# The last 64 queries of each pair as four-quarter fp32 score products, and a planner with other durations and another order

## The chip, the core and the metric

The kernel runs on one core of a Trainium2 chip. The metric is device time in microseconds (us). Five engines work side by side: TensorE (PE: matrix products; PEld is its loading of weights), VectorE (DVE), ScalarE (ACT), GpSimd (POOL) and SyncE (SP, which here issues DMA transfers). Each runs its own list of instructions in order and waits on semaphores for the others.

## The reference

Attention with pairwise averaged queries, then two mixer blocks. Only the attention stage is touched by the change.

```python
# q, k, v: (4, 8, 1152, 64) float32
q_pool = q.reshape(B, H, S // 2, 2, D).mean(axis=3)              # 576 queries
scores = scale * np.matmul(q_pool, k.transpose(0, 1, 3, 2))     # 576 x 1152
scores = scores - np.max(scores, axis=-1, keepdims=True)
attn = np.exp(scores)
attn = attn / (np.sum(attn, axis=-1, keepdims=True) + 1e-09)
attn_out = np.matmul(attn, v)
...
x = _moe_ref(x=x, **moe_kwargs)     # gelu, layer norm, gate over the sequence
return _moe2_ref(x=x, **moe2_kwargs)    # token mixing, then channel mixing
```

## The kernel before

**The work.** The 32 heads are taken as 16 pairs, two heads in the two halves of the 128 partitions. For each pair the queries (576 per head) and keys (1152 per head) are transposed on TensorE (`q_tr`, L459, and `k_tr`, L470, into the buffer `tt`). ScalarE and VectorE then split them into a high and a low fp32r part (`k_hi`, `k_lo`, `q_hi`, `q_lo`); a product is made of three passes, high by high, high by low and low by high.

The maximum of each query over its keys must be known before the exponentials. So the scores are computed twice. First (`scores`, L523, tile `s`) with queries on the output partitions: five tiles of queries, four of 128 and one of 64, by three groups of 384 keys, so 15 tasks of six products per pair. `rowmax` (L530, VectorE) reduces each to negated maxima `mx`. `least` (L537) combines the three groups, and the result is split into `nmz`, transposed (`nm_tr`, L553) and copied to `nmT`. Then (`turned`, L578, tile `sT`) with keys on the partitions, 9 tiles of 128 keys for each half of the queries: three passes and a fourth that adds the negated maximum. ScalarE takes the exponential (`expo`, L586, tile `e`), GpSimd adds the nine up (`total`, L592, tile `acc`), and TensorE multiplies them with the values (`av`, L601, tile `po`: fp32, one head in each column half). The column sums of `acc` (`sums`, L614, tile `pt`, fp32 too) give the denominators; ScalarE adds eps, VectorE takes the reciprocal (L625) and multiplies (L632).

**The order.** All tasks go into a `Plan`: each has an engine, a duration, predecessors, an urgency, and rings of buffers that it takes or gives back. The planner plays them forward with these durations and writes out each engine's order. TensorE's order is fixed by hand in `line()`; the planner only slips in weight transposes that have no place in it. Ring `s` is the one to watch: three PSUM buffers, shared by `tt`, `s` and `sT`. A task on TensorE that needs the next buffer waits until all readers of the buffer three tasks earlier are done.

TensorE works one pair ahead with the maxima: in the period of pair i it computes the turned scores of pair i, in six groups of three (T), and the 15 score tasks of pair i+1 (S) in five groups of three, each after a T group; values (A, three key tiles, so six fp32 products) follow one group behind. The key and query transposes (Q) of pair i+2 and the maxima's transpose (N) stand in the same period:

```python
out += at(*(("t", i, x, j) for j in range(3 * n, 3 * n + 3)))
out += maxima(i + 1, 3 * g, 3 * g + 3) if i else begin[g]
```

The fifth S group holds the 64-query tasks. In the front (pair 0) the order differs, since the maxima of pairs 0 and 1 must both be made there. Beside attention, VectorE, ScalarE and GpSimd convert weights for the later stages (`Piece`, steps `wz`, `wy`, `wd`; `wg` are transposed gate weights).

## Time and profile before

| | |
|---|---|
| Median of three runs | 1132.81 us (1127.57, 1132.81, 1132.83) |
| Profiled execution, its own time | 1127.43 us |
| Its span | 1125.6 us |
| Mean granted clock of TensorE over the span | 0.995 |
| Attention, to the first product of the next stage | 0 to 530.98 us |
| Later stages | 530.98 to 1125.6 us |

The profiled execution is one of its own, so its time stands beside the three. A task's cost on TensorE is best read as the time from its first product's start to that of the next task, since products overlap and the busy time of one includes its way through the array.

### The profile page before, as it was taken

The page shows a single profiled execution, that of the slowest core. Times are in us where ns is not written, and L with a number is a line of the kernel's source. Part 1 is how long each engine was busy: PE and PEld are TensorE (multiplying, and loading weights), DVE is VectorE, ACT ScalarE, POOL GpSimd, SP SyncE. Part 2 cuts the span into 40 slices and gives each one's busy share as a digit, 9 for nine tenths or more (in the row PEclk, how much of TensorE's full clock was granted, in tenths as well). Part 3 has the DMA queues.
Part 4 walks back from the last instruction along what each step waited for, and adds up shares of the span by engine and source line. Part 5 has one row for each costly group of instructions (what it writes and reads, how often), then busy time and mean ns, then how long its engine had stood idle before and what let it go on. Part 6 is the DMA issues. An engine that isn't in the chain of part 4 may idle for free.

```text
span 1125.6 us, 20953 instructions
## 1 busy us (share of the span) xinstructions
PE 1108.6 (98%) x8699; PEld 902.1 (80%) x8699; DVE 669.5 (59%) x884; ACT 464.8 (41%) x812; POOL 582.1 (52%) x423
## 2 busy tenths in 40 slices
PE   8999999999999999999999999999899999999998
PEld 6777777677777777776889999998888888888887
DVE  6778888877667687862878878875733202112121
ACT  2355556554544555545555544553434111111111
POOL 3688889988877788789274454431404202001000
PEclk8999999999999999999999999999999999999999
DMA  8322334334133433221721222126351100001010
GB/s 181 70 64 61 83 84 105 77 102 110 53 80 96 109 86 87 59 78 39 228 74 51 101 76 75 48 71 230 133 195 47 38 1 29 10 1 38 1 38 19
DMA packets 87918, 88.00 MB, mean 78 GB/s; under 512 B 42512, under 2 KB 71440, under 8 KB 86032
## 3 DMA queue, kind: packets, MB, share of 16 engines
q1 hardware_dynamic: 87824, 86.67, 26.6%
q8 instruction: 68, 1.11, 0.4%
q14 instruction: 26, 0.21, 0.1%
HBM read 66.70 MB, written 19.96 MB: 77 GB/s over the span
## 4 chain that ended last, share of the span: by engine, by line
PE 93%; DVE 4%; issue 1%; ACT 1%; DMA 1%; SPq 0%; DVEq 0%; ACTq 0%
PE sT L578 15%; PE po L601 13%; PE psc L1455 13%; PE po L1485 13%; PE s L523 11%; PE psO L1243 5%; PE psS L1194 4%; PE psV L1065 4%; PE psU L1165 4%; PE psK L1348 2%; PE tt L470 2%; PE psH L1372 2%; DVE mx L530 2%; PE pt L614 1%; PE tt L459 1%; PE tt L553 1%
## 5 line engine op out<-in xcount | busy, mean ns | idle before, releaser
L592 POOL TENSOR_TENSOR acc<-acc,e 128x576 f32<-128x576 f32 x224 | 320.4, 1430 | 71.0 <-ACT e L586 57.9
L530 DVE TENSOR_REDUCE mx<-s 128x2 f32<-128x768 f32 (+1 forms) x240 | 215.3, 945 | 95.6 <-PE s L523 95.6
L586 ACT ACTIVATE e<-sT 128x576 f32<-128x576 f32 x288 | 169.0, 652 | 88.0 <-PE sT L578 86.5
L578 PE MATMUL sT<-q,k 64*128 64x288 f32 x1728 | 166.0, 303 | 0.3
L578 PEld LDWEIGHTS sT<-q,k 64*128 64x128 f32 x1728 | 128.2, 184 | 42.3 <-DVE mx L530 15.6
L601 PE MATMUL po<-e,vn 128*64 128x288 f32 x1152 | 160.8, 414 | 0.0
L1341 DVE SCALAR_TENSOR_TENSOR gc<-psc,gc 128x512 fp32r<-128x512 f32 (+1 forms) x52 | 34.9, 671 | 208.3 <-ACT gc L1338 208.3
L523 PE MATMUL s<-k,q 64*128 64x384 f32 (+1 forms) x1440 | 146.0, 343 | 1.0 <-ACT q L479 0.7
L523 PEld LDWEIGHTS s<-k,q 64*128 64x128 f32 (+1 forms) x1440 | 110.0, 177 | 19.3 <-DVE mx L530 2.8
L1338 ACT ACTIVATE gc<-psc 128x512 fp32r<-128x512 f32 (+1 forms) x52 | 30.3, 582 | 219.0 <-PE psc L1455 209.3
L601 PEld LDWEIGHTS po<-e,vn 128*64 128x64 f32 x1152 | 74.3, 136 | 57.7 <-issue 17.1
L1485 PE MATMUL po<-wc,gc 128*128 128x512 f32 x408 | 99.7, 392 | 0.0
L1485 PEld LDWEIGHTS po<-wc,gc 128*128 128x128 f32 x408 | 76.4, 188 | 17.4
L578 PE MATMUL sT<-nmT,pick 64*128 64x288 f32 x576 | 85.3, 291 | 0.0
L625 DVE RECIPROCAL pt<-pt 128x288 f32<-128x288 f32 x32 | 62.8, 1962 | 30.4 <-ACT pt L621 30.2
L1194 PE MATMUL psS<-wsg,vn 128*128 128x288 f32 x448 | 60.9, 295 | 1.3 <-DVE gt L1220 1.3
L1194 PEld LDWEIGHTS psS<-wsg,vn 128*128 128x128 f32 x448 | 59.7, 188 | 1.7 <-DVE gt L1220 1.5
L1455 PE MATMUL psc<-x,wc 128*128 128x512 f32 (+1 forms) x288 | 59.1, 357 | 0.0
L257 POOL TENSOR_TENSOR vn<-gv,vn 128x512 fp32r<-128x512 f32 (+1 forms) x20 | 28.2, 1438 | 55.5 <-ACT vn L1155 55.1
L592 POOL TENSOR_TENSOR acc<-e 128x576 f32<-128x576 f32 x32 | 47.6, 1489 | 15.1 <-ACT e L586 14.9
L257 POOL TENSOR_TENSOR ws<-wz,ws 128x512 fp32r<-128x512 f32 x24 | 32.7, 1374 | 43.8 <-ACT ws L323 43.7
L1455 PEld LDWEIGHTS psc<-x,wc 128*128 128x128 f32 x288 | 47.8, 188 | 8.9
(131 smaller groups left out, 1730.9 us busy)
## 6 DMA issues: line engine op xcount, KB each, us to landing
ws<-in_moe_w_ch_dram SPq DMA_DIRECT2D x24, 512.0 KB, 4.0
qn<-in_q_dram SPq DMA_DIRECT2D x32, 288.0 KB, 5.2
kn<-in_k_dram SPq DMA_DIRECT2D x32, 288.0 KB, 4.2
vn<-in_v_dram SPq DMA_DIRECT2D x32, 288.0 KB, 3.2
ac<-ws SPq DMA_DIRECT2D x32, 256.0 KB, 2.6
wc<-ac SPq DMA_DIRECT2D x6, 1024.0 KB, 7.9
out_dram<-ob SPq DMA_DIRECT2D x18, 256.0 KB, 2.0
ws<-in_moe_w_in_dram SPq DMA_DIRECT2D x8, 512.0 KB, 5.6
```

The costliest lines, as they stand in the source:

```text
L257: eng.tensor_tensor(out=out_, in0=in0, in1=in1, op=ALU.subtract)
L523: nc.tensor.matmul(ps[0:m, h, 0:KC], flat(c.q[x])[r, t * P:t * P + m], c.k[y][r, cs], start=(n == 0), stop=(n == 2))
L530: nc.vector.tensor_reduce(out=mx[i % 2][0:m, t, :, g], in_=ps[0:m, :, 0:KC], axis=AX.X, op=ALU.max, negate=True)
L578: nc.tensor.matmul(ps[:, h, 0:TC], left, right, start=(n == 0), stop=(n == 3))
L586: nc.scalar.activation(out=s.e[j], in_=ps[:, :, 0:TC], func=AF.Exp)
L592: eng.tensor_tensor(out=s.acc, in0=s.e[0] if j == 1 else s.acc, in1=s.e[j], op=ALU.add)
L601: nc.tensor.matmul(s.po[D * h:D * h + D, 0:TC], c.vn[:, h, j], s.e[j][:, h], start=(j == 0), stop=(j == J - 1))
L625: nc.vector.reciprocal(out=s.den, in_=s.den)
L1194: nc.tensor.matmul(ps[:, ch, 0:TC], V[sx][:, ti, db * P:(db + 1) * P], L.ws[sw][:, ti, ch * TC:(ch + 1) * TC], start=first, stop=end)
L1243: nc.tensor.matmul(ps[:, ch, 0:TC], L.wo[sw][:, db, cb * P:(cb + 1) * P], L.g[sx][:, db, ch * TC:(ch + 1) * TC], start=first, stop=end)
L1455: nc.tensor.matmul(ps, W[WC1[f // 4]][sw][:, cc, (f % 4) * P:(f % 4 + 1) * P], u[sx][:, cc], start=first, stop=end)
L1485: nc.tensor.matmul(pos[i, tt], g[i, f][sx][:, tt * P:(tt + 1) * P], W[WC2[f // 4]][sw][:, f % 4], start=(f == 0 and n == 0), stop=(f == NF ...
```

## The change

Four things change.

The three tasks for the last 64 queries of a pair become two. `quarters` computes them as plain fp32 products with 64 queries as the weights: two heads in the two row halves of TensorE, and two ranges of 288 keys in the two column halves, so each of the four products of a task uses one quarter. `quartermax` reduces 128 x 576 scores, and `least` first folds the two column halves of the maxima together. For these products ScalarE makes unsplit copies of the transposed keys (`k_all`, tile `kf`) and of the 64 queries (`q_all`, tile `qf`), from the same `tt` buffers as the split parts.

`line()` becomes strings, one letter for a task or a pair of transposes: the quarters (X) stand behind the third A of a period, ahead of the fourth T group, and the third T group has no S group behind it any more. Keys are transposed ahead of queries (before: after them, but for pair 0). Pair 0's order is written anew.

The split of the maxima goes to ScalarE (`nm_hi`) for all pairs, where before VectorE did it in `both` for all but pair 0. The planner gets other durations, with the part after which a unit is free told apart from the landing of the result (`land`), and other lags. That changes the order on VectorE, ScalarE and GpSimd. The warm-up on TensorE grows from 13 to 18 products.

```diff
@@ class Plan
+    STALL = 0.0
...
-                    if not line or line[0]["mode"] != "r" and "tr" not in line[0]["take"]:
+                    if not line or line[0]["mode"] not in ("r", "x") and "tr" not in line[0]["take"]:
...
+                if at > free.get("PE", 0.0) + 1e-6:
+                    t["end"] += self.STALL
@@ attention
         plan = Plan()
+        plan.LAG, plan.TURN, plan.STALL = 0.08, 0.17, 0.05
         marks = {}
-        for name, n in dict(s=3, po=1, tr=1, e=10, acc=3, qn=1, qs=1, kn=1, vn=2, k=3, q=3,
-                            nm=2, nmT=2, os=2, den=2).items():
+        for name, n in dict(s=3, po=1, tr=1, e=10, acc=3, qn=1, qs=1, kn=1, vn=2, k=3, q=3, kf=2,
+                            nm=2, nmT=1, os=2, den=2).items():
...
+            c.kf = p2.tile([P, S], F32, tag="kf", name="kf", bufs=2)
+            c.qf = p2.tile([P, 2, D // 2], F32, tag="qf", name="qf", bufs=2)
...
+        def k_all(i, j0, j1, pt):
+            cs, x = k_cols(j0, j1, pt)
+            nc.scalar.copy(ctxs[i].kf[:, cs], x)
+
+        def q_all(i, pt):
+            _, ps = q_view(i, 0, pt)
+            nc.scalar.activation(
+                out=ctxs[i].qf, in_=ps[:, J - 2:J, 1], func=AF.Copy, scale=1.0 / 16)
...
+        def quarters(i, a):
+
+            c = ctxs[i]
+            ps = ps_s.tile([P, 2, 512], F32, tag="s", name="s4", bufs=3)
+            x = c.qf.rearrange("c j p -> c (j p)")
+            for n in range(2):
+                for h in range(2):
+                    r = slice(D * h, D * h + D)
+                    k0 = (2 * a + n) * TC
+                    nc.tensor.matmul(
+                        ps[D * n:D * n + D, h, 0:TC], x[r], c.kf[r, k0:k0 + TC],
+                        start=True, stop=True)
+            return ps
+
+        def quartermax(i, a, ps):
+            nc.vector.tensor_reduce(
+                out=mx[i % 2][:, NST - 1, :, a], in_=ps[:, :, 0:TC], axis=AX.X, op=ALU.max,
+                negate=True)
@@ least
+            if t1 == NST:
+                x = mx[i % 2][:, NST - 1]
+                nc.vector.tensor_reduce(
+                    out=x[0:TAIL, :, 2], in_=x[TAIL:P, :, 0:2], axis=AX.X, op=ALU.min)
@@ tasks
+            ka = [plan.add("ACT", 0.02 + 0.107 * (j1 - j0),
+                           lambda key=key, j0=j0, j1=j1: k_all(i, j0, j1, box[key]), land=0.12,
+                           after=[t_], urgency=u + 2.15, give=[("s", t_)])
+                  for j0, j1, key, t_ in ((0, J - 1, "k", kt), (J - 1, J, "q", qt))]
+            ka.append(plan.add("ACT", 0.15, lambda: q_all(i, box["q"]), after=[qt],
+                               urgency=u + 1.05, give=[("s", qt)], land=0.12))
...
-            todo = [(t, g) for t in range(NST) for g in range(3)]
+            todo = [(t, g) for t in range(NST - 1) for g in range(3)]
...
-                    x_ = plan.add("DVE", 0.99, lambda t=t, g=g: rowmax(i, t, g, box["s", t, g]),
+                    x_ = plan.add("DVE", 0.865, land=0.08, fn=lambda t=t, g=g: rowmax(i, t, g, box["s", t, g]),
...
+            for a in range(2):
+                at = base - 40 + 28 * (12 + a) / 15
+                s_ = pe["s", i, 12 + a] = plan.add(
+                    "PE", 0.48, put(("s", NST - 1, a), quarters, i, a), after=ka, urgency=at,
+                    take=["s"], mode="x", give=[("kf", kt)], land=0.16)
...
-                for e, d, f in (("ACT", 0.3, nm_hi), ("DVE", 0.4, nm_lo)) if first else ():
+                for e, d, f in (("ACT", 0.1, nm_hi), ("DVE", 0.28, nm_lo)):
@@ line
+        FRONT = "QSSSSSSSSSQN"
+        LINE = ("TTTSSSXXTTTSSSSNAXXTTTASSSSTTTQASSSSTTTATTTNA",
+                "TTTSSSATTTSSSATTTAXXTTTSSSQATTTSSSATTTNA",
+                "TTTATTTDATTTATTTATTTATTTDAAD")
...
+            order = FRONT + LINE[0] + LINE[1] * (NPAIR - 2) + LINE[2]
@@ attention, at its end
-        for _ in range(13):
+        for _ in range(18):
             nc.tensor.matmul(pt[:, 0:P], ident, ident, start=True, stop=True)
```

What this does to the orders, at three places. Line numbers after the change are some 30 higher.

TensorE, in the period of pair 1, around the 64-query tasks for pair 2. Before (the three `s` rows stand three times, once for each group of keys; `x2` is the two heads):

```order
L578 MATMUL sT<-nmT,pick 128x288 x2
L523 MATMUL s<-k_1098,q_1100 64x384 x2
L523 MATMUL s<-k_1099,q_1100 64x384 x2
L523 MATMUL s<-k_1098,q_1101 64x384 x2
...
L601 MATMUL po<-e,vn 64x288 x6
L614 MATMUL pt<-acc,ones 64x288 x2
L578 MATMUL sT<-q_628,k_626 128x288 x2
```

After:

```order
L611 MATMUL sT<-q_309,k_292 128x288 x2
L611 MATMUL sT<-nmT,pick 128x288 x2
L634 MATMUL po<-e,vn 64x288 x6
L547 MATMUL s_1002<-kf,qf 64x288 x4
L547 MATMUL s_1007<-kf,qf 64x288 x4
L611 MATMUL sT<-q_308,k_292 128x288 x2
L611 MATMUL sT<-q_308,k_293 128x288 x2
```

Eighteen fp32r products between turned scores and values became eight fp32 ones between values and turned scores, and turned scores are here followed by values directly.

VectorE, in the front, where the keys and queries of pair 2 (`k_626`, `q_628`; after: `k_620`, `q_639`) are split, and the maxima of pair 1 (`mx_110`) are reduced. Before:

```order
L530 TENSOR_REDUCE mx_110<-s 128x2 x9
L485 SCALAR_TENSOR_TENSOR q_629<-tt,q_628 128x288 x2
L257 TENSOR_TENSOR k_627<-tt,k_626 128x128
L257 TENSOR_TENSOR k_627<-tt,k_626 128x1024
L530 TENSOR_REDUCE mx_110<-s 128x2 x2
L530 TENSOR_REDUCE mx_110<-s 64x2 x3
```

After:

```order
L559 TENSOR_REDUCE mx_110<-s 128x2 x4
L261 TENSOR_TENSOR k_621<-tt,k_620 128x1024
L485 SCALAR_TENSOR_TENSOR q_640<-tt,q_639 128x288 x2
L559 TENSOR_REDUCE mx_110<-s 128x2 x2
L261 TENSOR_TENSOR k_621<-tt,k_620 128x128
L559 TENSOR_REDUCE mx_110<-s 128x2 x2
L567 TENSOR_REDUCE mx_110<-mx_110 64x2
```

The subtraction of the last 128 keys (`128x128`) moved behind two reductions, and the long one ahead of the queries'.

ScalarE, in a steady period, where keys and queries have been transposed into `tt`. Before:

```order
L846 CAST wg<-pt 128x512
L479 ACTIVATE q_4810<-tt 128x9x2x32
L505 CAST k_4808<-tt 128x128
L505 CAST k_4808<-tt 128x1024
L608 COPY os<-po 128x288
L586 ACTIVATE e<-sT 128x576 x3
```

After:

```order
L887 CAST wg<-pt 128x512
L506 CAST k_4286<-tt 128x1024
L479 ACTIVATE q_4304<-tt 128x9x2x32
L518 ACTIVATE qf<-tt 128x64
L506 CAST k_4286<-tt 128x128
L514 COPY kf<-tt 128x1024
L514 COPY kf<-tt 128x128
L641 COPY os<-po 128x288
L619 ACTIVATE e<-sT 128x576 x3
```

The long key cast moved ahead of the queries', and the copies to `qf` and `kf` stand between the casts and the output copy `os`.

## Rows read from the trace of the kernel before

**Rows 1.** The page: busy time and share of the span, and instructions.

```profile
PE 1108.6 (98%) x8699; PEld 902.1 (80%) x8699; DVE 669.5 (59%) x884; ACT 464.8 (41%) x812; POOL 582.1 (52%) x423
```

**Rows 2.** Windows by stage: length, busy us (instructions) by engine, clock, DMA.

```profile
23.39:59.41 36.02, 35.36 (x361) 25.47 (x360) 25.56 (x34) 15.35 (x28) 25.58 (x17) 1.00 0.36 82
59.41:509.65 450.24, 448.29 (x4727) 332.53 (x4725) 344.33 (x405) 237.09 (x425) 375.58 (x255) 1.00 0.32 85
...
530.98:1125.60 594.62, 585.29 (x3274) 513.39 (x3272) 281.09 (x414) 194.87 (x328) 155.72 (x130) 1.00 0.21 71
```

**Rows 3.** Timeline of TensorE, pair 5: start us, us, line, out<-in, count.

```profile
177.86 0.67 PE L578 MATMUL sT<-q,k 64*128 64x288 f32 x6
...
178.49 0.57 PE L578 MATMUL sT<-q,k 64*128 64x288 f32 x6
...
179.56 1.73 PE L523 MATMUL s<-k,q 64*64 64x384 f32 x18
181.22 1.68 PE L601 MATMUL po<-e,vn 128*64 128x288 f32 x12
...
183.31 0.66 PE L578 MATMUL sT<-q,k 64*128 64x288 f32 x6
...
185.65 1.68 PE L601 MATMUL po<-e,vn 128*64 128x288 f32 x12
187.26 0.66 PE L578 MATMUL sT<-q,k 64*128 64x288 f32 x6
...
188.94 1.80 PE L523 MATMUL s<-k,q 64*128 64x384 f32 x18
190.66 1.68 PE L601 MATMUL po<-e,vn 128*64 128x288 f32 x12
```

**Rows 4.** Timeline of TensorE, last pair.

```profile
509.65 0.66 PE L578 MATMUL sT<-q,k 64*128 64x288 f32 x6
...
511.43 1.68 PE L601 MATMUL po<-e,vn 128*64 128x288 f32 x12
```

**Rows 5.** Groups by shape, 60 to 520 us: busy us, mean ns.

```profile
L586 ACT ACTIVATE e<-sT 128x576 f32<-128x576 f32 x261 | 152.9, 652 | 76.2 <-PE sT L578 74.7 <-POOL acc L592 1.5
L530 DVE TENSOR_REDUCE mx<-s 128x2 f32<-128x768 f32 x168 | 150.9, 944 | 66.6 <-PE s L523 66.6
...
L601 PEld LDWEIGHTS po<-e,vn 128*64 128x64 f32 x1044 | 67.3, 136 | 52.4 <-issue 15.7 <-DMA vn<-in_v_dram 0.5
...
L307 DVE SCALAR_TENSOR_TENSOR wz<-wz,wy 128x512 int32<-128x512 int32 x12 | 17.0, 1415 | 1.1 <-ACT wy L285 0.9
...
L505 ACT CAST k<-tt 128x1024 fp32r<-128x1024 f32 x13 | 13.2, 1013 | 1.3
...
L505 ACT CAST k<-tt 128x128 fp32r<-128x128 f32 x13 | 3.4, 259 | 0.0
```

**Rows 6.** Timeline of all engines where keys and queries are transposed.

```profile
205.22 2.69 DVE L530 TENSOR_REDUCE mx<-s 128x2 f32<-128x768 f32 x3 [1.83 <-PE s L523]
...
206.23 0.77 PE L459 MATMUL tt<-ident,qs 64*128 64x64 f32 x9
...
209.72 0.67 PE L578 MATMUL sT<-q,k 64*128 64x288 f32 x6
...
210.62 1.74 ACT L586 ACTIVATE e<-sT 128x576 f32<-128x576 f32 x3 [0.39 <-PE sT L578]
```

**Rows 7.** Window of the longest steady period.

```profile
187.26:221.07 33.81, 31.91 (x339) 23.68 (x337) 28.94 (x32) 18.52 (x33) 32.17 (x23) 1.00 0.32 85
```

**Rows 8.** Timeline of TensorE in the front.

```profile
50.06 3.36 PE L523 MATMUL s<-k,q 64*128 64x384 f32 x30
53.36 1.68 PE L601 MATMUL po<-e,vn 128*64 128x288 f32 x12
```

**Rows 9.** Timeline of TensorE at the start.

```profile
1.35 5.61 PE L921 MATMUL tt<-ident 128*128 128x128 f32 x26 [1.35 <-POOL ident masks.py:199]
8.66 1.06 PE L470 MATMUL tt<-ident,kn 128*128 128x128 f32 x8 [1.70 <-DMA kn<-in_k_dram]
```

More of the change, by code (lines that the diff above doesn't have):

```diff
@@ L449, in attention @@
         K8 = T + D
-        def new_k(c):
-            c.k = [p2.tile([P, S], F32R, tag=f"k{r}", name=f"k{r}", bufs=3) for r in range(2)]
         def q_tr(i):
@@ L491, in k_tr @@
             pt = big()
-            if not i:
-                new_k(c)
             for j in range(J - 1):
                 k_tr1(c, pt, j * P, j)
+            c.k = [p2.tile([P, S], F32R, tag=f"k{r}", name=f"k{r}", bufs=3) for r in range(2)]
+            c.kf = p2.tile([P, S], F32, tag="kf", name="kf", bufs=2)
+            c.qf = p2.tile([P, 2, D // 2], F32, tag="qf", name="qf", bufs=2)
             return pt
@@ L656, in tasks @@
             qa = plan.add(
-                "DVE" if first else "POOL", 1.4 if first else 2.7,
-                lambda: q_add(i, nc.vector if first else nc.gpsimd), after=lq, urgency=u - 4,
+                "DVE" if first else "POOL", 1.3 if first else 2.6,
+                lambda: q_add(i, nc.vector if first else nc.gpsimd), after=lq, urgency=u - 4, land=0.08,
                 take=["qs"], give=[("qn", lq[0])])
-            qt = pe["q", i] = plan.add("PE", 0.75, put("q", q_tr, i), after=[qa, *lk], urgency=u + 1,
-                          take=["s", "q"] + ([] if first else ["k"]), give=[("qs", qa), ("kn", lk[0])], mode="t")
@@ L662, in tasks @@
-            kt = pe["k", i] = plan.add("PE", 0.9, put("k", k_tr, i), after=lk, urgency=u + 2,
-                          take=["s"] + (["k"] if first else []), give=[("kn", lk[0])], mode="t")
+            qt = pe["q", i] = plan.add("PE", 0.75, put("q", q_tr, i), after=[qa, *lk], urgency=u + 1, land=0.16,
+                          take=["s", "q"], give=[("qs", qa), ("kn", lk[0])], mode="t")
+            kt = pe["k", i] = plan.add("PE", 0.9, put("k", k_tr, i), after=lk, urgency=u + 2, land=0.16,
+                          take=["s", "k", "kf"], give=[("kn", lk[0])], mode="t")
@@ L680, in tasks @@
+            l_ = plan.add("DVE", 0.85, lambda: q_lo(i, box["q"]), after=[h_], urgency=u + 1, land=0.08,
                           give=[("s", qt)])
@@ L688, in tasks @@
                     need = ready + kr[g]
-                    s_ = pe["s", i, m] = plan.add("PE", 0.53, put(("s", t, g), scores, i, t, g), after=need,
+                    s_ = pe["s", i, m] = plan.add("PE", 0.54, put(("s", t, g), scores, i, t, g), after=need, land=0.16,
                                   urgency=at, take=["s"], mode="r")
                     marks[max(at, 0)] = s_
-                    x_ = plan.add("DVE", 0.99, lambda t=t, g=g: rowmax(i, t, g, box["s", t, g]),
+                    x_ = plan.add("DVE", 0.865, land=0.08, fn=lambda t=t, g=g: rowmax(i, t, g, box["s", t, g]),
@@ L693, in tasks @@
                                   after=[s_], urgency=at - 5, give=[("s", s_)])
                     maxed.append(x_)
+            for a in range(2):
[3 more added lines that the diff above has]
+                    take=["s"], mode="x", give=[("kf", kt)], land=0.16)
+                maxed.append(plan.add(
+                    "DVE", 0.67, lambda a=a: quartermax(i, a, box["s", NST - 1, a]),
+                    after=[s_], urgency=at - 5, give=[("s", s_)], land=0.08))
@@ L695, in tasks @@
             nms, nts = [], []
             for n, (t0, t1) in enumerate(((0, 3), (3, NST)) if first else ((0, NST),)):
-                def both(n=n, t0=t0, t1=t1):
-                    nm = least(i, t0, t1)
-                    nc.vector.tensor_copy(nmz[i % 2][:, t0:t1, :, 0], nm)
-                    nm_lo(i, t0, t1, nm)
-                lm = plan.add("DVE", 0.3 if first else 0.75,
-                              put(("m", n), least, i, t0, t1) if first else both,
+                lm = plan.add("DVE", 0.3 if t1 == NST else 0.1, put(("m", n), least, i, t0, t1), land=0.08,
@@ L711, in tasks @@
+                own["last"].append(("nm", lm))
                 nt = pe["n", i, n] = plan.add(
-                    "PE", 0.1 + 0.09 * (t1 - t0), put(("n", n), nm_tr, i, t0, t1), after=[lm],
-                    urgency=base - 8, take=["s"] + ([] if n else ["nmT"]),
-                    give=[] if first else [("nm", lm)], mode="t")
+                    "PE", 0.1 + 0.09 * (t1 - t0), put(("n", n), nm_tr, i, t0, t1), after=[lm], land=0.16,
+                    urgency=base - 8, take=["s"] + ([] if n else ["nmT"]), mode="t")
@@ L781, in tasks @@
                     pe["d", i, x] = plan.add(
-                        "PE", 0.5, this["go"], after=[prev], urgency=at + 2,
+                        "PE", 0.47, this["go"], after=[prev], urgency=at + 2, land=0.16,
                         take=["tr"], give=[("acc", own)], late=last, mode="c")
@@ L912, in attention @@
             have = [t for i in range((2 if ti == CC else 1) * NP) for t in outs[i]]
-            h = plan.add("ACT", 0.62, lambda ti=ti: x_high(0, ti), after=have, urgency=400.0 + 10 * ti)
+            h = plan.add("ACT", 0.5, lambda ti=ti: x_high(0, ti), after=have, urgency=400.0 + 10 * ti)
             plan.add("POOL", 1.4, lambda ti=ti: x_low(0, ti, nc.gpsimd), after=[h],
```

111 lines of the change are left out of this document (47 added, 64 removed).

## The prediction

> **What bounds the kernel now.** I read the page first, then the windows by stage, TensorE's timeline through one pair, and the groups of instructions by shape. The page gives TensorE 98% of the span [rows 1]. [...] After 530.98 the engines' orders are the same in both kernels to the last instruction, so I leave 594.62 us alone. Everything is decided ahead of that.
>
> The timeline shows how steady the sequence is [rows 3]. The last 64 queries of the next pair are the group at 179.56: 18 half-height products, 1.66 us until the next group starts. A full-height group of three (188.94 to 190.66) takes 1.72: 64 queries cost as much as 128. Changing the kind of product costs too. The first turned task of a group takes 0.63 (177.86 to 178.49), the two behind it 0.54 each (to 179.56). Six fp32 products before turned scores take 1.61 (185.65 to 187.26). With two sums behind them they take 2.09 in all (181.22 to 183.31), so the two add 0.48, which is the price of two fp32 products on the two column halves side by side; the six alone are then 1.45, and 0.16 is the change of kind. One excursion into fp32 and back thus costs 0.2 to 0.3.
>
> **The steady pairs, term by term.** There are 14 periods between 59.41 and 509.65.
>
> (a) Removed: a turned group and the 64-query group, 177.86 to 181.22, 3.36 us, become a turned group that goes straight to the weighted values. The last pair shows that form: 509.65 to 511.43, 1.78 [rows 4]. That is -1.58 us per pair.
>
> (b) Added: two tasks of four fp32 products of 288 columns. No row shows four quarters at work. The nearest is the pair of sums: two products on two halves, 0.48. If the four run beside each other as those two do, a task is 0.48; if only two can, it is 0.97. Nothing shorter than 0.48 is likely, since each quarter streams the same 288 columns. [...] I take both splits to hold together, 0.97 us for the two tasks, and keep 1.94 for the range.
>
> (c) The two tasks stand between fp32 values and turned scores, so there is one more change of kind. From the 0.1 and 0.16 above I take 0.2, from 0.1 to 0.3. [...]
>
> (d) The key transposes now come first, then the nine of q, then the one key transpose that shares their buffer: one more change of row height, between nothing and the 0.1 above; I take 0.05.
>
> Sum: -1.58 + 0.97 + 0.2 + 0.05 = -0.36 us per pair, -5.0 us over 14.
>
> **Off the path.** VectorE loses three reductions of 768 columns, 944 ns each [rows 5], and a small cast per pair, and gains two of 576 columns, between 0.71 (by columns) and 0.94: about 1 us or more of slack. The cast's work, now on ScalarE, costs at most the 259 ns of a 128-column copy. ScalarE also gets plain copies of the keys, priced as the casts of that shape, 1013 and 259 ns, and one of the queries, at most 259: under 2 us more on about 17 of 32. Neither is near TensorE.
>
> The copies do hold two of the three score buffers longer, so I walk that place. Before, q's transposes start at 206.23, and the three turned tasks behind them and the values at 209.72 [rows 6]. In the new order ScalarE has: key cast, q cast, small q copy, small key cast, then both plain key copies, then the output copy and the exponentials. Queued instructions follow each other some 0.11 closer than their mean (three exponentials of 652 ns take 1.74 [rows 5, 6]). Starting 1.2 us after the first transpose, the long key copy ends at 1.2 + 0.90 + 0.54 + 0.15 + 0.15 + 0.90 = 3.84, and its buffer is wanted by the second turned task, at 209.72 + 0.63 - 206.23 = 4.12. The other buffer waits for the small copy, 3.99, and for VectorE: score reductions until 1.68 (207.91), long key subtraction 2.2 to 3.4, q to 4.2, small key subtraction to 4.5; wanted by the third turned task, 0.54 on, at 4.66. Nothing stalls, but the margin is 0.1 to 0.3 us. In VectorE's order, of the 13 pairs that have this place two have two weight conversion steps of 1.4 us each [rows 5] around the score reductions, between the new reductions and the small key subtraction. There the buffer comes up to 1.4 late, less what slack stands ahead; I put it at 0.75 us for each of the two, +1.5, from nothing to 2.8. Before shows that such steps can stall TensorE: it idles 1.95 us in the whole stretch [rows 2], 1.9 of it at once, behind VectorE in the period from 187.26, which takes 33.81 against a mean of 32.16 [rows 7].
>
> **The front, 23.39 to 59.41.** TensorE has six score tasks fewer (0.52 each, as (1.72 - 0.16) / 3, so 3.1) and four new ones (1.94) with three changes of kind (0.6): -0.6. But VectorE's order is worse at one place: two reductions of 0.87 us (three take 2.69 [rows 6]) now stand ahead of the small key subtraction, which alone releases the buffer that the third score task of the row needs. Before, both key subtractions stood ahead of them. While they run TensorE waits, 1.75 us. Before, the same stretch lost its time in small waits, as the group of five scores at 50.06 which took 3.30 instead of 5 x 0.52 + 0.16 = 2.76 [rows 8]. Five more warm-up products are 10 more instructions of 0.21 (5.61 / 26), or half that once the clock is full: done at 9.0 at the latest, likely at 8.0, while the keys are waited for until 8.66 [rows 9]. At most 0.4 is lost. Together +1.0, between -1 and +2.5.
>
> **Sum.** -5.0 + 1.5 + 1.0 = -2.5 us on the profiled 1127.43, which is its span of 1125.6 and 1.8 around it. The median of the three runs shown is 1132.81, 5.4 above the profile and 5.2 above the fastest, so these runs scatter by more than the whole change. Against the median: 1130.3.
>
> **Rivals.**
> *Nothing is given back.* The stalls I charge do not come, since VectorE has more slack in every pair: -5.0, or -7.8 if the change of kind in (c) costs nothing too, so 1125.0 to 1127.8 against the median. For it: TensorE's one stall in 14 periods before. Against it: the margins of 0.1 to 0.3 above.
> *Two quarters at a time.* Same-row quarters take turns. Then (b) is 1.94, every pair is 0.61 slower than before, and 16 pairs add 15.5 us to my sum: 1145.8, slower than before. It decides from 0.66 us per task on: there the pair gains nothing. For it: no row shows four. Against it: both kinds of halves run side by side, and the weight loads of the values, two halves in the same 128 rows, lie beside each other: 1044 of 136 ns fill 67.3 us, not 142 [rows 5]. [...]
> *The buffers come free late.* If the plain copies from the score buffer are 0.3 us slower than the casts, each pair stalls 0.5 to 1 us after the key transposes: 1137 to 1144. It starts once the long copy ends 4.1 us after the first transpose. Against it: the same shape and source as the casts.
>
> **Chances.** Four quarters at once with part given back 0.48; nothing given back 0.25; two at a time 0.16; late buffers 0.11. Half a percent, 5.7 us, is about what a measurement of this kernel can tell from no change. The first case lies within it but for 0.04 below; the second is mostly beyond; late buffers split 0.04 to 0.07. So faster 0.29, same 0.48, slower 0.23. The likeliest case alone spans 1126 to 1134. Leaving out the worst of both ends gives 1122 to 1142.
>
> **What would show it.** In the profile of the changed kernel: two groups of quarters per pair, 0.48 us from one to the next, and about 1.2 us from the first to the turned scores; steady periods about 0.36 us shorter, a mean of 31.8 to 31.9 instead of 32.16; the last pair's first scores at 506 to 508. A wait of some 1.8 us in the second half of the front, ahead of pair 1's third last score task. After the key transposes the second and third turned task on time. Wrong would be 0.97 per task, a mean period over 32.2 with TensorE waiting on a key copy or subtraction, or a front more than 3 us longer.

## The result, and the profile after

The changed kernel takes 1135.45 us (median of 17 runs, 1134.09 to 1140.4), the kernel before on the same chips 1128.84 (17 runs, 1127.11 to 1133.38): a ratio of 1.0053, interval 1.004 to 1.0066. It is half a percent slower, 6.6 us; the forecast was 1130.3, which is 2.5 us less than the 1132.81 that it was reckoned from, and "same". The profiled execution takes 1134.34 us, its span is 1132.5.

The page, to set beside [rows 1]:

```profile
PE 1110.8 (98%) x8677; PEld 896.7 (79%) x8677; DVE 649.3 (57%) x869; ACT 483.6 (43%) x875; POOL 583.3 (52%) x423
```

TensorE is still all of it (98%, and in the steady stretch below 449.69 of 453.84 us at a granted clock of 1.00, as before [rows 2]), VectorE has 20 us less to do and ScalarE 19 more. The windows of the same three stages, to set beside [rows 2] (length, busy us and instructions of PE, PEld, DVE, ACT and POOL, TensorE's clock, DMA share, GB/s):

```profile
24.61:62.39 37.78, 36.85 (x357) 26.19 (x357) 24.38 (x32) 17.18 (x34) 23.79 (x17) 0.95 0.30 71
62.39:516.23 453.84, 449.69 (x4699) 328.08 (x4697) 325.27 (x393) 252.33 (x477) 377.54 (x255) 1.00 0.32 84
537.67:1132.50 594.83, 585.17 (x3272) 513.22 (x3272) 280.73 (x414) 194.49 (x328) 155.32 (x129) 1.00 0.21 71
```

Three things lost time: the first turned product starts 1.22 us later (24.61, was 23.39), the front takes 1.76 longer (37.78, was 36.02), and the 14 steady periods take 453.84 instead of 450.24, though they should have become shorter. The later stages are as before (594.83, was 594.62). 1.22 + 1.76 + 3.60 = 6.6 of the span's 6.9.

The quarters themselves do what was forecast. TensorE's timeline in one pair, to set beside [rows 3] (start us, us, line, out<-in, count):

```profile
74.67 1.68 PE L634 MATMUL po<-e,vn 128*64 128x288 f32 x12
76.27 1.20 PE L547 MATMUL s<-kf,qf 64*64 64x288 f32 x16
77.40 0.68 PE L611 MATMUL sT<-q,k 64*128 64x288 f32 x6
```

From 76.27 to 77.40 it is 1.13 us for both tasks and the change of kind; 0.97 + 0.2 had been the sum. (Why from start to start: in the trace of before, products of 512 columns start 0.23 us apart and last 0.39 each, `psc` from 1016.11 on, and products of 288 columns start 0.13 apart and last 0.29, `psO` from 700.07 on; both last 0.16 longer than the distance.) The loss lies three groups on, where keys and queries are transposed. All engines there, to set beside [rows 6] (in brackets the idle time before an instruction and who ended it):

```profile
112.94 1.09 PE L470 MATMUL tt<-ident,kn 128*128 128x128 f32 x8
...
115.11 1.23 DVE L261 TENSOR_TENSOR k<-tt,k 128x1024 fp32r<-128x1024 f32 x1 [0.50 <-ACT k L506]
115.58 0.22 ACT L518 ACTIVATE qf<-tt 128x64 f32<-128x64 f32 x1
115.68 0.27 ACT L506 CAST k<-tt 128x128 fp32r<-128x128 f32 x1
...
116.37 1.18 ACT L514 COPY kf<-tt 128x1024 f32<-128x1024 f32 x2 [0.42 <-DVE k L261]
...
116.53 0.67 PE L611 MATMUL sT<-q,k 64*128 64x288 f32 x6
...
117.44 0.67 PE L611 MATMUL sT<-q,k 64*128 64x288 f32 x6
...
117.58 0.29 DVE L261 TENSOR_TENSOR k<-tt,k 128x128 fp32r<-128x128 f32 x1 [0.52 <-ACT kf L514]
```

ScalarE has nothing left to do from about 115.9 and could start the plain copy of the keys, but VectorE is still reading the same buffer for its subtraction, until 116.34. The copy starts at 116.37, and the second turned product, which needs the buffer, at 117.44 instead of 0.53 after the first. Then the small subtraction waits in its turn for the small copy. The waits of the steady stretch say that this is every pair (waiting line, what ended it, us in total, times, longest):

```profile
DVE k L261 <- ACT kf L514: 6.7, 13, 0.5
ACT kf L514 <- DVE k L261: 5.5, 13, 0.4
...
PEld sT L611 <- ACT kf L514: 4.5, 13, 0.4
```

The turned group behind the key transposes takes 2.09 to 2.11 us in all 13 pairs that have that place, where it took 1.70 before. The copies are not slow in themselves; the groups by shape (busy us, mean ns) have them as the casts of [rows 5]:

```profile
L514 ACT COPY kf<-tt 128x1024 f32<-128x1024 f32 x13 | 13.2, 1015 | 5.5 <-DVE k L261 5.5
L506 ACT CAST k<-tt 128x1024 fp32r<-128x1024 f32 x13 | 13.2, 1013 | 16.8 <-PE tt L470 16.8
```

So the program keeps readers of one PSUM buffer on different engines apart (PSUM is where the matrix products of these kernels land; SBUF, below, is where their other tiles lie): from pair 1 on, in the traces of before and of the changed kernel, no read of a buffer `tt` by ScalarE overlaps a read of the same buffer by VectorE. Why it keeps them apart no run shows.

### The profile page after: what moved, and what is told of

The parts are those of the page before. It is cut to its first block, busy times and chain, and to the rows that moved or that the text cites. A ratio compares the mean times of both kernels' runs of the same rounds, so it can differ in the third digit from the quotient of the medians.

```text
span 1132.5 us, 20988 instructions
## 1 busy us (share of the span) xinstructions
PE 1110.8 (98%) x8677; PEld 896.7 (79%) x8677; DVE 649.3 (57%) x869; ACT 483.6 (43%) x875; POOL 583.3 (52%) x423
## 4 chain that ended last, share of the span: by engine, by line
PE 84%; DVE 9%; ACT 4%; DMA 2%; issue 1%; SPq 0%; DVEq 0%; ACTq 0%
PE po L1516 13%; PE psc L1486 13%; PE sT L611 13%; PE po L634 10%; PE s L533 7%; PE psO L1274 4%; PE psS L1225 4%; PE psV L1096 4%; PE psU L1196 3%; DVE mx L559 3%; PE psK L1379 2%; PE psH L1403 2%; DVE k L261 2%; ACT kf L514 1%; PE s L547 1%; PE tt L470 1%
## 5 line engine op out<-in xcount | busy, mean ns | idle before, releaser
L559 DVE TENSOR_REDUCE mx<-s 128x2 f32<-128x768 f32 x192 | 172.3, 951 | 92.9 <-PE s L533 92.7
L611 PE MATMUL sT<-q,k 64*128 64x288 f32 x1728 | 170.8, 308 | 5.2 <-ACT kf L514 1.7
L533 PE MATMUL s<-k,q 64*128 64x384 f32 x1152 | 118.8, 344 | 3.6 <-DVE k L261 1.1
L533 PEld LDWEIGHTS s<-k,q 64*128 64x128 f32 x1152 | 94.8, 187 | 15.6 <-DVE mx L559 3.2
L311 DVE SCALAR_TENSOR_TENSOR wz<-wz,wy 128x512 int32<-128x512 int32 (+2 forms) x42 | 52.7, 1254 | 4.1 <-ACT wy L289 2.5
```

The source lines that it names most:

```text
L311: nc.vector.scalar_tensor_tensor(out=zi, in0=zi, scalar=0x7FFFFFFF, in1=self.y, op0=ALU.bitwise_and, op1=ALU.bitwise_or)
L533: nc.tensor.matmul(ps[0:m, h, 0:KC], flat(c.q[x])[r, t * P:t * P + m], c.k[y][r, cs], start=(n == 0), stop=(n == 2))
L559: nc.vector.tensor_reduce(out=mx[i % 2][0:m, t, :, g], in_=ps[0:m, :, 0:KC], axis=AX.X, op=ALU.max, negate=True)
L611: nc.tensor.matmul(ps[:, h, 0:TC], left, right, start=(n == 0), stop=(n == 3))
```

## The experiments

Theory A: the plain copies of the keys hold the score buffers, because they take turns with VectorE at one buffer. Rival B: the planner's new durations order VectorE and ScalarE worse. Rival C: the quarters, or ScalarE's added work in itself. The table has the ratio to the kernel before with its interval, and from each profile the start of the first turned product, the front from there to the first turned product of pair 1, and the 14 steady periods (to the first turned product of the last pair). Spans are those of the profiled executions.

| run | ratio | first turned | front | steady |
|---|---|---|---|---|
| before | 1 | 23.39 | 36.02 | 450.24 |
| changed kernel | 1.0053 (1.004 to 1.0066) | 24.61 | 37.78 | 453.84 |
| e1 | 1.0264 (1.0239 to 1.0289) | 23.34 | 44.18 | 474.85 |
| e2 | 0.9989 (0.9975 to 1.0003) | 23.21 | 36.74 | 449.38 |
| e3 | 1.0037 (1.0023 to 1.0052) | 26.45 | 38.89 | 449.71 |
| e4 | 1.0016 (0.9998 to 1.0035) | 23.32 | 35.77 | 452.57 |
| e5 | 1.002 (1.0007 to 1.0032) | 23.36 | 38.43 | 449.42 |
| e6 | 1.0209 (1.019 to 1.0229) | 24.62 | 37.25 | 470.36 |
| e7 | 1.0202 (1.0183 to 1.0221) | 23.75 | 37.82 | 469.50 |
| e8 | 1.0275 (1.0255 to 1.0294) | 23.72 | 37.69 | 477.07 |
| e9 | 1.0006 (0.9991 to 1.0021) | 23.33 | 36.74 | 450.50 |
| e10 | 1.0018 (1.0001 to 1.0034) | 23.19 | 36.66 | 450.67 |
| e11 | 0.9997 (0.9984 to 1.0011) | 26.03 | 38.45 | 445.78 |
| e12 | 0.9914 (0.9891 to 0.9936) | 23.78 | 38.38 | 436.16 |
| e13 | 0.9984 (0.9969 to 0.9999) | 23.34 | 36.67 | 445.71 |
| e14 | 0.9857 (0.9825 to 0.9888) | 24.64 | 38.78 | 428.48 |
| e15 | 1.0012 (0.9997 to 1.0027) | 25.25 | 36.91 | 449.65 |

**e1, the parts split in SBUF.**

```diff
-            nc.scalar.copy(ctxs[i].k[0][:, cs], x)
+            nc.scalar.copy(ctxs[i].k[0][:, cs], ctxs[i].kf[:, cs])
...
-            sub(nc.vector, ctxs[i].k[1][:, cs], x, f32(ctxs[i].k[0][:, cs]))
+            sub(nc.vector, ctxs[i].k[1][:, cs], ctxs[i].kf[:, cs], f32(ctxs[i].k[0][:, cs]))
```

> The changed kernel, but ScalarE's plain copies (k_all) are the first readers of the transposed keys, and the high and low parts are made from that copy in SBUF, so that each score buffer is let go after one reader (1.0 us) instead of three. If the score buffers come free late because the plain copy and VectorE's subtraction read one buffer and are kept apart (theory A), the turned group behind the key transposes goes from 2.10 back to about 1.70 us in all 13 pairs that have it (-5.3), the first turned group of pair 0 starts near 23.4 instead of 24.6 (-1.2), and the span falls by 5 to 8 us from 1132.5, to 1124.5 to 1127.5; the time is then 0.995 or so of the changed kernel. If the new planner durations and the order that they give VectorE and ScalarE lose the time (rival B), or the quarters themselves (rival C), the span stays at 1131 or more.

A miss: 1159.68 us. The start's wait is gone (23.34), but the turned group behind the key transposes takes 2.80 in most pairs and up to 5.12. VectorE's timeline shows why; the second fence is GpSimd's, around the same time:

```profile
123.22 2.36 DVE L261 TENSOR_TENSOR k<-kf,k 128x1024 fp32r<-128x1024 f32 x1 [1.58 <-ACT k L506]
...
498.05 1.23 DVE L261 TENSOR_TENSOR k<-kf,k 128x1024 fp32r<-128x1024 f32 x1 [1.57 <-ACT k L506]
```

```profile
121.85 2.64 POOL L443 TENSOR_TENSOR qs<-qn 64x1152 f32<-64x1152 f32 x1 [0.32 <-PE tt L461]
```

With both operands in SBUF the subtraction takes 2.36 us, where it takes 1.23 with one in PSUM. It ends 1.1 us after GpSimd's addition does, at 124.49, so it seems to have stood still until then; the one at 498.05, the only long one that no addition of GpSimd meets, takes 1.23 with the same operands. The experiment changed two things and decides nothing on A but the start.

**e2, no key copies.** The quarters read one constant tile, so the maxima of the last 64 queries are of constants.

```diff
-            c.kf = p2.tile([P, S], F32, tag="kf", name="kf", bufs=2)
+            c.kf = kf0
```

> The changed kernel without the plain key copies: the quarters read one constant tile, so the scores of each pair's last 64 queries are of constants. It leaves out 26 or so ScalarE copies (1.0 and 0.26 us) and keeps the quarters, the order on TensorE and the durations. Theory A: the turned group behind the key transposes takes about 1.70 us, first turned group near 23.4, span 1124 to 1127. Rival B or C: span 1131 or more, since the copies run on an engine with a third of its time idle.

The group takes 1.70 in 12 of the 13 pairs (1.89 once), the start is 23.21, the time that of the kernel before (the span, 1127.5, is 0.5 above what was expected). As A has it; but ScalarE's work was removed with the hold.

**e5, the copies kept, the hold removed.** The copies read the high parts in SBUF, so the maxima of the last 64 queries are of rounded keys.

```diff
-            nc.scalar.copy(ctxs[i].kf[:, cs], x)
+            nc.scalar.copy(ctxs[i].kf[:, cs], f32(ctxs[i].k[0][:, cs]))
```

> The changed kernel with ScalarE's extra key copies kept, in number, shape and engine, but read from the high parts in SBUF instead of from the score buffer: the quarters then see keys rounded to their high parts. The score buffer of the keys is let go after two readers instead of three. If it is the buffer held by the third reader that costs (theory A), the turned group behind the key transposes takes about 1.70 us as in the run without copies, the first turned group starts near 23.3, and the span is 1126 to 1129. If it is ScalarE's extra 1.27 us a pair in itself (rival C), the group stays at 2.0 us or more and the span at 1131 or more.

The timeline of all engines behind the transposes:

```profile
115.32 1.27 ACT L514 COPY kf<-k 128x1024 f32<-128x1024 f32 x2
115.75 0.81 DVE L485 SCALAR_TENSOR_TENSOR q<-tt,q 128x288 fp32r<-128x288 f32 x2
...
116.02 0.67 PE L611 MATMUL sT<-q,k 64*128 64x288 f32 x6
...
116.66 0.56 PE L611 MATMUL sT<-q,k 64*128 64x288 f32 x6
```

The same copies of the same length, and the group is back at 1.70 in all 13 pairs and the steady stretch at 449.42, where e2 has 449.38: the hold costs, not ScalarE's work. That decides between A and C for the steady stretch. The span is 1130.1, above what was expected: the front stayed long (38.43), since TensorE's clock was at half there (0.50 from 24 to 26 us), during the first turned group, which took 3.33 where it takes 1.68 in e13; its second and third task took 0.96 each, where the second takes 0.53 in e13.

**e3 and e4, the durations.** e3 is the changed kernel with all durations, lags and landings of the planner as before; e4 is the kernel before with the new ones. One line of some thirty:

```diff
-                x_ = plan.add("DVE", 0.865, land=0.08, fn=lambda t=t, g=g: rowmax(...
+                x_ = plan.add("DVE", 0.99, lambda t=t, g=g: rowmax(...
```

> The changed kernel's work and TensorE order, with the planner's durations, lags and landings of the kernel before, so that VectorE, ScalarE and GpSimd are ordered by them. Theory A: the stall behind the key transposes stays (2.0 to 2.2 us for that group), span within 2 us of 1132.5. Rival B (the new durations lose the time): the span falls to 1125 to 1128.

> The kernel before (no quarters, its TensorE order and work) with the new durations, lags and landings of the planner alone. Theory A: no change, within 0.2% of before. Rival B: slower than before by 4 to 7 us, the loss of the whole change and the quarters' gain beside it.

In e3 the stall behind the key transposes stays (2.07 to 2.11), as A has it. But the steady stretch is 4.13 us shorter than the changed kernel's, and the first turned product comes at 26.45. In e4 the steady stretch is 2.33 us longer than before from nothing but other durations, though its time is not told apart from before. So B is no alternative to A but a second loss, hidden in e3's time by a worse start.

**e6 to e8, other work behind the transposes.** In e6 the sums move from the first task of averages of a half to the last, so that they stand behind the key transposes:

```diff
-                    before = pend.pop() if pend and i < NPAIR - 1 and po is None else None
+                    before = pend.pop() if pend and i < NPAIR - 1 and js is AVG[-1] else None
```

> The changed kernel with one difference: the sums of the exponentials (four products, 0.5 us more in a task of the averages) ride on the last averages task of a half instead of the first, so that in each pair they stand right behind the key transposes and the averages task there, ahead of the turned group. Nothing is left out. Theory A: TensorE has 0.48 us of other work while the last copies free the buffer, so the turned group behind them takes 1.70 to 1.78 instead of 2.11, 4 to 5.3 us less in the steady stretch, span 1127 to 1129; the start keeps its wait of 1.66. If the wait were not for the buffers, the group would stay at 2.1 and the span at 1132 to 1133.

e7 adds that the first pair's plain keys are made by GpSimd from the parts in SBUF (`kf = k0 + k1`), e8 besides that the conversions have their old durations.

> The same with the plain keys of the first pair made by GpSimd as the sum of the high and the low parts in SBUF, while it idles, so that the first pair's score buffers are let go as in the kernel before. Theory A: besides, the first turned group starts near 23.3 instead of 24.6 and the front loses 1 to 2.5 us, span 1124.5 to 1127.5. If the start's wait has another cause, it stays near 24.6 and the span at that of the run before it.

> The same again with the planner's old durations for the conversion of the weights alone (seven numbers). The stalls near conversions summed to 5.7 us in the changed kernel, 2.7 before and about 1 with all the old durations: if these seven numbers decide it (rival B in part), the steady stretch loses 2 to 4 us more, span 1121 to 1124.5. If the stalls come from the order of other steps or from the quarters, it stays within 1 us of the run before it.

All three missed by 20 us and more. VectorE's timeline of e6 behind the transposes, with TensorE's next scores:

```profile
188.93 1.97 DVE L658 RECIPROCAL pt<-pt 128x288 f32<-128x288 f32 x1 [0.73 <-ACT pt L654]
...
191.47 0.26 DVE L261 TENSOR_TENSOR k<-tt,k 128x128 fp32r<-128x128 f32 x1
...
191.79 1.34 PE L533 MATMUL s<-k,q 64*128 64x384 f32 x12 [0.47 <-DVE k L261]
```

The sums bring their reciprocal along, and the small key subtraction, which gives a score buffer back, now stands behind it. TensorE has one buffer less until then: the turned group takes 2.47 to 2.49, and the score group behind it waits for the subtraction (last row). The two account for most of the 16.5 us by which the steady stretch is longer than the changed kernel's. e7's first turned product at 23.75 says again that the late start is the copies' hold; e8 says nothing, since its base was disturbed.

**e9 to e11, quarters on the high parts.** No copies at all: the quarters read the high parts that the other scores use. A maximum only shifts the exponents of its row, so rounded scores do.

```diff
-            x = c.qf.rearrange("c j p -> c (j p)")
+            x = f32(flat(c.q[0])[:, T - TAIL:T])
...
-                        ps[D * n:D * n + D, h, 0:TC], x[r], c.kf[r, k0:k0 + TC],
+                        ps[D * n:D * n + D, h, 0:TC], x[r], f32(c.k[0][r, k0:k0 + TC]),
```

e10 has the old durations for the conversions alone, e11 all old ones.

> The changed kernel whose quarters read the high parts of keys and queries, which are in SBUF for the other scores, so that the three plain copies a pair fall away altogether (the maxima of the last 64 queries are then of rounded scores; a maximum only shifts the exponents of a row). Theory A: as the run without key copies: the turned group behind the key transposes 1.70, first turned group near 23.2, span 1126 to 1128.5, 5 us or so under the changed kernel. The rest of the way to the predicted gain would be rival B's: stalls near conversions of about 6 us as in the runs with the new durations.

> The run before it with the old durations for the conversions of the weights alone. If these seven numbers make the conversion stalls (6 us there, 2.7 in the kernel before), the steady stretch loses 2 to 4 us and the span is 1122.5 to 1125.5; if not, within 1 us of the run before it.

> The quarters on the high parts, with all durations, lags and landings of the kernel before. Rival B, together with A: the steady stretch was 449.7 us with these durations and a stall of 0.39 a pair behind the key transposes, so 444 to 446 without that stall; the front may lose up to 3 us as it did with these durations (first turned group at 26.45). Span 1123 to 1127. If the stalls near conversions come from the quarters' shorter period instead, the steady stretch stays at 448 or more.

e9 is 5 us under the changed kernel, as A has it (its span, 1129.5, is 1.0 above what was expected). e10's steady stretch is e9's: the seven numbers of the conversions do not make the stalls. e11's is 4.72 shorter than e9's and within what was expected: all the durations together do. What e11 wins there it loses at the start. VectorE and GpSimd around 23 us:

```profile
21.96 1.23 DVE L261 TENSOR_TENSOR k<-tt,k 128x1024 fp32r<-128x1024 f32 x1 [0.30 <-ACT k L503]
...
22.73 2.60 POOL L442 TENSOR_TENSOR qs<-qn 64x1152 f32<-64x1152 f32 x1 [5.42 <-DMA qn<-in_q_dram]
23.10 2.26 DVE L261 TENSOR_TENSOR nmz<-nm,nmz 128x6 fp32r<-128x6 f32 x1
```

The old durations put pair 1's long key subtraction ahead of the small one for the maxima of pair 0. That costs not 1.2 but 2.7 us: the small one, 0.17 us long where it comes first, now meets GpSimd's addition and takes 2.26, to that addition's end.

**e13 and e15, the parts put together.** e13 is e11 with the first pair planned by the new durations, which moves that one subtraction back; e15 has the same order on VectorE in attention and the changed kernel's copies.

```diff
-            tasks(i)
+            (first_tasks if i < 1 else tasks)(i)
```

> The quarters on the high parts, the first pair planned with the new durations, all else with the durations of the kernel before. VectorE's order is then that of the run on old durations except for one subtraction of the first pair, which stands behind the small one of the maxima again. If the held buffers, the swap at the start and the order at the conversions make up the loss, the first turned group starts near 23.3, the front takes 36.7, the steady stretch 445.8, so that the last pair but one ends near 505.8 against 509.65 in the kernel before, and the time is 3 to 6 us under before (ratio 0.995 to 0.9975). If the front depends on more than that swap, the first turned group starts after 25 and the time is that of before.

> The same order on VectorE with the changed kernel's plain copies from the score buffers, so that the copies alone tell this run from the one before it. Theory A: stall of 0.4 behind the key transposes in 13 pairs and a later start: first turned group near 24.6, front 37.8, steady 449.7, together 6 to 6.5 us over the run without copies, 1.5 to 3 us over the kernel before. If the copies cost only together with the new order, it lies within 2 us of the run without them.

Windows of e13, then of e15:

```profile
23.34:60.01 36.67, 35.23 (x356) 24.60 (x356) 24.74 (x34) 15.35 (x29) 24.98 (x17) 1.00 0.35 80
60.01:505.72 445.71, 444.08 (x4700) 326.47 (x4698) 317.63 (x393) 237.81 (x438) 375.97 (x255) 1.00 0.33 86
```

```profile
25.25:62.16 36.91, 35.70 (x356) 24.59 (x356) 24.08 (x32) 17.07 (x34) 23.28 (x17) 1.00 0.32 74
62.16:511.81 449.65, 447.09 (x4699) 326.99 (x4698) 316.89 (x393) 252.49 (x477) 375.79 (x255) 1.00 0.33 85
```

The profile of e13 does to 0.1 us what was expected: 23.34, 36.67, 445.71, and the steady stretch ends at 505.72, 3.9 ahead of before. Its time is only 1.0 under before, less than the 3 to 6 expected: 1.5 us is given back in the later stages, below, and the profiled execution, at 1125.02, is the fastest of its 12 runs, 2.45 under their median. e15 starts 0.6 later than expected and ends at 511.81, 6.1 behind e13, and its time is 4.2 over e13's: the copies, in an order that is otherwise the same on VectorE and differs by the places of two exponentials on ScalarE and two pairs of neighbours on GpSimd. So the way from before to the changed kernel at the end of the steady stretch is -3.9 (quarters without copies, good order), +6.1 (copies), +4.4 (the new durations for all pairs, 516.23 - 511.81): +6.6. TensorE's clock blurs this a little in the front: between 12 and 18 us it has a stretch at half in e15 (0.50 from 14 to 16) and none in e13, which is some 0.6 of the 6.1 (the key transposes of pair 1 start at 20.57 in e15, and at 19.93 in the changed kernel, whose clock is full up to there). In the steady stretch it is 1.00 in all four, and there the parts are -4.5, +3.9 and +4.2.

**e12 and e14, one product for all maxima.** What holds for 64 queries holds for all: the first scores need only the high parts. e12 is e9, e14 is e13, with one product for three.

```diff
-            for n, (x, y) in enumerate(PASSES):
+            for n, (x, y) in enumerate(PASSES[:1]):
```

> The quarters on the high parts, and all other maxima from one product of high parts instead of three (again, only the shift of a row's exponents changes). Not about the cause, but about what the maxima need: 12 tasks a pair fall from 0.57 to about 0.2 us, so 4.5 us a pair if TensorE stays the bound; GpSimd is busy 26.9 us of each pair's 32, so no pair gets under 27. Between 30 and 60 us faster than the kernel before if the order holds, less if VectorE's reductions (12 times 0.9 and two of 0.75) become what TensorE waits for.

> The run with one product of high parts for all maxima, planned like e13. That run lost some 9 us near conversions in its steady stretch (436.2 where 15 undisturbed pairs would take some 427); with the old order there it should take 428 to 432, and the time is 6 to 9 us under that run's 1119.

e12 gains 0.9%, far less than the 30 to 60 us. A score group falls only from 1.72 to 1.37. Among the waits of e12's steady stretch one has grown, the scores' weight loads waiting for the exponentials, which give the score buffers back (1.5 us in the kernel before):

```profile
PEld s L531 <- ACT e L617: 41.9, 113, 0.7
```

So by these waits the buffers are the limit there, and the cut of the products shows only in part. e14 is 1112.56, 1.4% under before and the fastest here: the better order carries over, and is worth 6.5 us there.

## Why the prediction was wrong

**The terms of the sum, (a) to (d).** Right. e13's undisturbed periods are 31.58 to 31.60 us where those of before are 31.89: -0.30 against -0.36. The quarters run four at a time: in the pair above the first four of the sixteen instructions start between 76.27 and 76.30, the next four from 76.57 on. The rival with two at a time is out (1.13 us for both tasks with the change of kind, not 2.1). That row halves run beside each other, which the 0.97 of (b) takes, the trace of before shows for the scores: the 18 products from 179.56 on start two by two, at most 0.02 us apart, and the next two 0.17 to 0.18 later. (c) was 0.17 (1.13 less 2 x 0.48) instead of 0.2; what TensorE does in that time no run shows. (d) was 0.10 instead of 0.05 (1.98 from the first key transpose to the values, was 1.88). Not foreseen: 0.07 in the turned group behind the quarters (1.77, was 1.70).

**"Nothing stalls".** This is the step that failed, and with it the steady stretch went the other way. The walk added up ScalarE's queue and VectorE's queue each for itself and had the long key copy end 3.84 after the first transpose, 0.28 before it was wanted. Its queue was right: ScalarE was free at 3.0, where the walk has 2.94. But the copy reads the buffer that VectorE's subtraction reads, and had to wait until that ended, 3.4 after the first transpose in the walk's own numbers as in the trace. It ended near 4.5. The prediction had both instructions and both times and did not ask whether they may overlap. In place of no stall there is one of 0.4 us in each of 13 pairs, 3.9 us of the steady stretch (e15 against e13), and one of about 1 us at the start. The rival "the buffers come free late" names the place and the price (0.5 to 1 us; it is 0.41), but gave it 0.11 and hung it on a slower copy, which did not happen: 1015 ns against 1013.

**The conversions, +1.5.** Mis-sized, and at the wrong place. In the two pairs that the prediction means, with conversion steps on both sides of the score reductions (at 142 and 241 us), nothing comes later than elsewhere, though the steps are there and take 1.4 and 0.7 us: the turned groups behind the key transposes take 2.11 and 2.10 there as in all pairs. Two other pairs lose 0.9 each, 2.66 instead of 1.77, behind the quarters, whose reductions stand behind a conversion step:

```profile
172.97 1.55 DVE L317 SCALAR_TENSOR_TENSOR wz<-wz,wd 128x512 f32<-128x512 f32 x1
...
174.44 1.41 DVE L553 TENSOR_REDUCE mx<-s 128x2 f32<-128x576 f32 x2
...
175.25 0.67 PE L611 MATMUL sT<-q,k 64*128 64x288 f32 x6 [0.56 <-DVE mx L553]
```

That 2 x 0.9 is near 2 x 0.75 is luck; e13 and e15, with the old durations, have the two places too. Missing is what the new durations do elsewhere: 4.2 us of the steady stretch (453.84 - 449.65). The changed kernel and e15 around one conversion:

```profile
192.14 0.67 ACT L295 ACTIVATE wd<-ws 128x512 int16<-128x512 f32 x1
...
192.85 0.63 ACT L299 ACTIVATE wd<-wd 128x512 f16<-128x512 int16 x1
...
193.38 1.72 ACT L619 ACTIVATE e<-sT 128x576 f32<-128x576 f32 x3
...
194.63 1.44 POOL L625 TENSOR_TENSOR acc<-e 128x576 f32<-128x576 f32 x1 [0.61 <-ACT e L619]
...
194.68 1.94 DVE L317 SCALAR_TENSOR_TENSOR wz<-wz,wd 128x512 f32<-128x512 f32 x1
...
196.54 2.67 DVE L559 TENSOR_REDUCE mx<-s 128x2 f32<-128x768 f32 x3
```

```profile
191.77 1.74 ACT L618 ACTIVATE e<-sT 128x576 f32<-128x576 f32 x3 [0.30 <-PE sT L610]
...
193.38 0.68 ACT L295 ACTIVATE wd<-ws 128x512 int16<-128x512 f32 x1
193.67 2.67 DVE L558 TENSOR_REDUCE mx<-s 128x2 f32<-128x768 f32 x3
...
196.26 0.78 DVE L317 SCALAR_TENSOR_TENSOR wz<-wz,wd 128x512 f32<-128x512 f32 x1
```

With the new durations the conversion's casts stand ahead of three exponentials, and its last step ahead of three reductions; with the old ones behind them. The score buffers wait for both, and this one place costs 1.5 us (the period takes 33.45, e15's 31.96). Much of that is not order alone: the last step takes 1.94 us in the changed kernel and 0.78 in e15. Both its inputs are in SBUF, and it ends 0.55 after GpSimd's addition of 194.63 does, as ten of the twelve such steps of the changed kernel in attention end 0.55 after an addition; the other two take 0.68. The prediction looked at conversion steps only around the key subtraction, and took the durations, which were read from traces, for harmless. Which of them decides is open: the conversions' own seven do not (e10).

**The front, +1.0.** Right for what it counted: e13's front, without copies, is 36.67, +0.65. The wait forecast at 1.75 ahead of pair 1's late score tasks is there with 1.2 in the changed kernel (a group of four takes 3.41 where 4 x 0.52 + 0.16 is 2.24). The five more warm-up products cost nothing: they follow each other by 0.21 us up to 5.57 and by 0.11 from 5.72 on (the trace's first entry for the clock, 1.00, is at 5.63), and end at 7.67, while the keys are waited for until 8.82. Missing is the hold at the start, where the walk was not made. TensorE waits 1.66 for it, where it waits 0.57 in e13, and then, from about 26 us on, its clock falls:

```profile
24.61 0.66 PE L611 MATMUL sT<-q,k 64*128 64x288 f32 x6 [1.66 <-ACT kf L514]
```

```profile
24.00:26.00 2.00, 1.39 (x18) 1.27 (x20) 0.54 (x2) 1.50 (x4) 1.47 (x1) 1.00 1.15 247
26.00:28.00 2.00, 2.00 (x18) 2.00 (x16) 0.07 (x1) 1.45 (x3) 1.12 (x1) 0.53 0.59 152
28.00:30.00 2.00, 2.00 (x20) 1.54 (x22) 2.00 (x3) 0.00 (x0) 1.71 (x2) 0.62 0.74 148
30.00:32.00 2.00, 2.00 (x32) 1.38 (x24) 2.00 (x3) 0.36 (x1) 0.00 (x0) 1.00 0.00 0
```

At this clock (0.50 from 27 to 29 us) the score group from 26.73 on takes 2.94 us; in e13, at 1.00, it takes 1.75. That the wait brings the half clock is not shown: e15 waits 1.67 at the same place and keeps the full clock, 1.00, to the end of the front. The kernel before had its half clock earlier, between 10 and 17 us (0.50 from 10 to 16), among the first score tasks.

**The whole.** 1135.45 lies in the range of 1122 to 1142, above the 1126 to 1134 of the likeliest case. It lies there by luck, not because the account held: the upper end stood for other causes, slower copies or quarters that take turns. As a change, -2.5 was forecast and +6.6 came. Of the 9.1 between them 7.1 arose in the steady stretch (+3.6 where -5.0 + 1.5 was forecast) and 2.0 up to its start (+3.0 where +1.0 was).

## What to carry to other kernels

Before you give a buffer another reader, list all its readers by engine: on PSUM they take turns in this program, and the buffer is held for their sum, however idle the engine of the new one is (0.4 us in each of 13 pairs here, with ScalarE idle for 0.42 ahead of the copy). Ask next whether the reader is needed; here the copies served a maximum for which a rounded copy already in SBUF does. A planner with truer durations gives another order, not a better one: measure the order by itself before it travels with another change.

## What the runs showed that was not expected

In these runs VectorE loses up to 3.4 us on an instruction with both inputs in SBUF while GpSimd adds (the longest long subtraction of e1 takes 4.67, the one without an addition 1.23), and nothing on the long subtraction with an input in PSUM. The subtraction of 128x6 takes 0.17 us alone and 2.26 in e11, ending 0.03 us after GpSimd's addition; the long one takes 2.36 in e1, and 1.23 with PSUM while GpSimd adds beside it (115.11 in the changed kernel, GpSimd from 114.82 on). The conversion steps above, with both inputs in SBUF too, go the same way (ten of twelve end 0.55 us after an addition). Why VectorE takes longer there no run shows.

The later stages do not always keep what attention wins. The prediction left them alone, since the orders there are the same. In e13 TensorE waits once near the end, for a VectorE instruction behind an addition that itself waits for an output transfer:

```profile
1088.86 1.34 PE L1624 MATMUL psc<-x,wc 128*128 128x256 f32 x9 [1.60 <-DVE uc L1510]
```

The wait is 1.6 to 2.2 us in the profiles of e2, e5 and e9 to e14, all without copies from the score buffers, 0.3 to 0.7 in the changed kernel, e3, e6 to e8 and e15, and not there in before, e1 and e4. Why, among the kernels with quarters, it is longer where no copy reads the score buffers, some 570 us after attention's last, stays open; no run was made on it.
